# Two ways to lay 256 rows of w2 over partitions and DMA engines in a decode kernel

## The chip, the cores and the metric

The kernel runs on one core of one Trainium2 chip. The metric is the device time of one execution in microseconds (us). Before the change it is 134.84 us, the median of 6 runs between 134.77 and 134.99. The profile comes from one execution of 134.82 us; its span, from the first to the last instruction on the core, is 133.0 us. Times inside the execution are counted from the start of the span.

## What is computed

Two branches read the same layer-normalised input `xn` of shape (2, 1, 576), and their sum with the residual is the output. Branch A is attention of a single token over the last 2048 of 8192 cached positions. Branch B is a two-layer MLP with a squared ReLU.

```python
def _A_ref(x, k_cache, v_cache, wq, wo):
    W = min(4096, max(256, Sk // 4))                    # 2048
    q = (x @ wq).reshape(B, Sq, Hq, Dh) ...             # 32 heads of 128, 16 kv heads
    scores = jnp.einsum("bhqd,bhkd->bhqk", q, k) * (Dh ** -0.5)
    o = jnp.einsum("bhqk,bhkd->bhqd", _softmax(scores), v)
    return o.reshape(B, Sq, Hq * Dh) @ wo               # wo: 4096 x 576

def _B_ref(x, w1, b1, w2, b2):
    h = jnp.einsum("bsd,df->bsf", x, w1) + b1           # w1: 576 x 4608
    r = jnp.where(h > 0, h, 0)
    return jnp.einsum("bsf,fd->bsd", r * r, w2) + b2    # w2: 4608 x 576

xn = _layernorm(x)
return x + _A_ref(xn, ...) + _B_ref(xn, ...)
```

Everything is bf16. All caches and weights that are used are read once: 53.62 MB from HBM.

## The kernel before

The 2 x 16 pairs of batch and kv head are worked through in eight units `u` of four kv heads. A unit's K and its V are 2 MB each and lie in a pool of six tiles, `kvpool`, which later also holds w2. For each unit `step` (line 518) transposes K on TensorE (`transposes`, line 315, read back by ACT and DVE at lines 327 and 329), computes scores and the softmax, and does the product with V of the unit two steps earlier. After the last unit come the MLP's first layer (`mlp_h_start` to `mlp_h_end`), the last two V products, wo and w2, then the final addition (line 594) and the store (line 595).

All large loads are issued by SyncE (SP), in an order written out by hand: K of unit 0, wq, K and V of the units, then `issue_wo(0)`, w1, the last two V, `issue_wo(1)`, and w2 in six pieces (`W2P`, line 510, loaded by `issue_w2`, line 164, whose `dma_start` is line 173). An SP load is issued when its buffer is free and when an earlier DMA that used the same completion semaphore has landed; DMAs of SP and ACT take eight semaphores in turn. Each of these loads has 128 partitions, so each of the core's 16 DMA engines gets eight rows of it.

w2 has 4608 rows of 576 numbers (1152 bytes each). They are divided into four groups of `HW` = 1152 rows. In the first three groups a partition holds `FR` = 9 neighbouring rows. In the last group, 896 rows are laid over 128 partitions with `FT` = 7 rows each, and the remaining 256 rows are "extra" rows that `XS` (line 74) describes. An entry of `XS` is (rows in a partition, partitions, partitions of one DMA):

```python
    def issue_w2x():
        if x_parts:
            s, i = x_parts.pop(0)
            xr, xp, xe = XS[s]
            rows = B_w2[FX[s]:FX[s] + xr * xp, :].rearrange("(e i r) n -> i e (r n)", e=xe, r=xr)
            tc.keep_in_program_order(nc.scalar.dma_start(out=w2x_sb[s][i:xp:xp // xe, :], in_=rows[i]))
```

So an entry is loaded by xp / xe DMAs of xe partitions each, with one contiguous run of xr rows for each partition. ScalarE (ACT) issues them (line 186), one at each call of `issue_w2x`, and `load_k` and `load_v` call it from unit 3 and unit 1 on. Before the change, (3, 32, 8) makes four DMAs of 8 partitions with 3456 bytes each, and (8, 20, 5) makes four DMAs of 5 partitions with 9216 bytes each. ACT also issues the loads of x, b1 (4 partitions of 2304 bytes) and b2 (1152 bytes), and the store of the output.

The extra rows are used by `mlp_x` (line 491): two matmuls for each row index, 2 x (3 + 8) = 22 in all, which contract over 32 or 20 partitions. `mlp_h_end` (line 447) transposes the activations into the same layout, with one small transpose for each entry of `CX` (7 + 3 + 8 = 18) and one copy for each of the three layouts (line 467). The last two pieces of w2 are used by `mlp_tail` (line 479), whose result `tail_ps` goes into the final addition.

Of the kernel before, what the change touches and what calls it, by code (L numbers as in the profile page):

```python
# [16 lines left out]
def kernel(  # L17
# [53 lines left out]
    HW = F // NG4  # L71
    HB = HW // 3
    FR = HW // P
    XS = ((3, 32, 8), (8, 20, 5))
    FT = (HW - sum(r * p for r, p, _ in XS)) // P
    F3 = (NG4 - 1) * HW
    CX = [(r, FT, P) for r in range(FT)]
    FX = []
    for xr, xp, _ in XS:
        FX.append(F3 + FT * P + sum(m * n for m, n, _ in XS[:len(FX)]))  # L80
        CX += [(FX[-1] - F3 + r, xr, xp) for r in range(xr)]
    assert FX[-1] + XS[-1][0] * XS[-1][1] == F
    N3 = (NG4 - 1) * FR
# [92 lines left out]
    const.tile([P, 96], F32, name="pad_0")  # L176
    w2x_sb = [const.tile([xp, xr * D], BF16, name=f"w2x_sb_{i}") for i, (xr, xp, _) in enumerate(XS)]
    const.tile([P, 24], F32, name="pad_1")
    x_parts = [(s, i) for s, (_, xp, xe) in enumerate(XS) for i in range(xp // xe)]

# [445 lines left out]
```

## Time and profile before

| quantity | value |
|---|---|
| median of 6 runs | 134.84 us (134.77 to 134.99) |
| the profiled execution | 134.82 us, span 133.0 us |
| busy: PE / DVE / ACT / POOL | 88.7 / 58.6 / 46.9 / 5.4 us |
| bytes moved by DMA | 53.74 MB, 404 GB/s over the span |
| mean granted TensorE clock | 0.879 |
| ACT-issued DMAs for the extra rows | 4 of 45.0 KB, 4 of 27.0 KB |
| matmuls on the extra rows (`mlp_x`) | 22, from 112.0 us on, 404 to 443 ns each |
| last piece of w2: issued at, landed at | 107.59, 129.65 us |
| store of the output issued at | 130.38 us |

The busy shares of the compute engines say how much work each has, not what sets the end. For that one reads the chain of work that ended last, and then the stage in which it ends. The DMA row of the profile is a mean over 16 DMA engines that each work off their own share; the queue table names who asked for the bytes: q1 is SP's queue, q10 is ACT's, and the queues of kind "instruction" bring the engines' own program code.

### The profile page before, as it was taken

The page shows a single profiled execution, that of the slowest core. Times are in us where ns is not written, and L with a number is a line of the kernel's source. Part 1 is how long each engine was busy: PE and PEld are TensorE (multiplying, and loading weights), DVE is VectorE, ACT ScalarE, POOL GpSimd, SP SyncE. Part 2 cuts the span into 40 slices and gives each one's busy share as a digit, 9 for nine tenths or more (in the row PEclk, how much of TensorE's full clock was granted, in tenths as well). Part 3 has the DMA queues.
Part 4 walks back from the last instruction along what each step waited for, and adds up shares of the span by engine and source line. Part 5 has one row for each costly group of instructions (what it writes and reads, how often), then busy time and mean ns, then how long its engine had stood idle before and what let it go on. Part 6 is the DMA issues. An engine that isn't in the chain of part 4 may idle for free.

```text
span 133.0 us, 2082 instructions
## 1 busy us (share of the span) xinstructions
PE 88.7 (67%) x850; PEld 52.5 (39%) x850; DVE 58.6 (44%) x160; ACT 46.9 (35%) x65; POOL 5.4 (4%) x18
## 2 busy tenths in 40 slices
PE   0069546988697477678497597497815495927970
PEld 0059214465353244344253353265402153314640
DVE  6725305244584574394367584574400423062010
ACT  5717303178294256256084184463200400000010
POOL 7000000010100100100100100100100000000000
PEclk9999985569999999999999999999996865555797
DMA  4999999999999999999999999999999999999940
GB/s 124 422 417 446 424 434 433 424 429 430 419 443 412 443 428 423 434 431 426 434 424 443 424 438 424 429 438 421 432 423 433 434 432 420 433 407 436 407 184 1
DMA packets 4458, 53.74 MB, mean 404 GB/s; under 512 B 551, under 2 KB 682, under 8 KB 1230
## 3 DMA queue, kind: packets, MB, share of 16 engines
q1 hardware_dynamic: 4320, 53.32, 94.4%
q10 hardware_dynamic: 130, 0.31, 0.6%
q8 instruction: 6, 0.10, 0.3%
q14 instruction: 2, 0.02, 0.0%
HBM read 53.62 MB, written 0.00 MB: 403 GB/s over the span
## 4 chain that ended last, share of the span: by engine, by line
DMA 92%; PE 3%; DVE 1%; SPq 1%; issue 0%; DVEq 0%
DMA v<-in_A_v_cache_dram 43%; DMA k<-in_A_k_cache_dram 20%; DMA w<-in_B_w_dram 17%; DMA wq<-in_A_wq_dram 12%; PE kT_ps L110 2%; PE o_ps L107 1%; SPq L128 0%; DVE kT L329 0%; SPq L135 0%; DVE o L386 0%; DVE o L388 0%; DVE fin_sb L594 0%; PE tail_ps L107 0%; DVEq L594 0%
## 5 line engine op out<-in xcount | busy, mean ns | idle before, releaser
L110 PE MATMUL kT_ps<-ident_f,k 128*128 128x128 f32 x256 | 39.4, 298 | 12.4 <-DMA k<-in_A_k_cache_dram 9.7
L110 PEld LDWEIGHTS kT_ps<-ident_f,k 128*128 128x128 f32 x256 | 30.7, 152 | 25.8 <-issue 13.6
L327 ACT COPY kT<-kT_ps 128x1024 bf16<-128x1024 bf16 x32 | 31.7, 1013 | 19.7 <-PE kT_ps L110 18.8
L329 DVE COPY kT<-kT_ps 128x1024 bf16<-128x1024 bf16 x32 | 21.8, 682 | 16.4 <-PE kT_ps L110 16.4
L107 PE MATMUL sc_ps<-kT,qz 128*32 128x512 bf16 x128 | 10.5, 413 | 5.8 <-DVE kT L329 5.8
L359 ACT ACTIVATE p<-sc_ps,bias 128x512 bf16<-128x512 f32 x8 | 5.5, 687 | 17.9 <-DVE gown L355 14.4
L107 PE MATMUL o_ps<-v,pT 128*32 128x512 bf16 x128 | 11.2, 445 | 0.0
L588 ACT COPY part<-out_ps 17x144 f32<-17x144 f32 x2 | 0.5, 268 | 23.8 <-DVE part L588 23.8
L348 DVE TENSOR_REDUCE m<-sc_ps 128x1 f32<-128x512 f32 x8 | 5.5, 692 | 7.2 <-PE sc_ps L107 7.2
L388 DVE SCALAR_TENSOR_TENSOR o<-o_ps,in_s,o 128x128 f32<-128x128 f32 x24 | 8.3, 347 | 0.5
L362 DVE STREAM_TRANSPOSE pT<-p 128x512 bf16<-128x512 bf16 x8 | 5.7, 710 | 6.4 <-ACT p L359 6.4
L107 PEld LDWEIGHTS <-xnT 128*2 128x2 bf16 x100 | 2.6, 96 | 11.8 <-issue 10.8
L107 PE MATMUL out_ps<-wo,ws 128*17 128x288 bf16 x64 | 6.1, 365 | 1.6 <-DVE ws L421 1.6
L352 POOL PARTITION_ALL_REDUCE gmax<-m x8 | 2.9, 367 | 88.3 <-DVE m L350 88.3
L386 DVE TENSOR_SCALAR o<-o_ps,in_s 128x128 f32<-128x128 f32 x8 | 2.7, 343 | 8.6 <-PE o_ps L107 8.5
L107 PE MATMUL h_ps<-w,xnT 128*2 128x384 bf16 x48 | 3.2, 421 | 4.9 <-DMA w<-in_B_w_dram 4.9
L107 PE MATMUL op_ps<-o,of_h 128*128 128x129 f32 x16 | 4.0, 338 | 3.3 <-DVE o L388 3.2
L107 PEld LDWEIGHTS <-qz 128*32 128x32 bf16 x128 | 2.2, 98 | 10.0 <-DVE kT L329 7.4
L107 PEld LDWEIGHTS <-hT_sb 128*17 128x17 bf16 (+2 forms) x104 | 4.6, 100 | 3.7 <-issue 1.4
L453 DVE TENSOR_TENSOR hrow<-t 98x384 bf16<-98x384 f32 x3 | 1.6, 556 | 8.3 <-ACT t L452 8.2
L107 PEld LDWEIGHTS <-ws 128*17 128x17 bf16 x64 | 3.7, 112 | 3.8 <-DVE ws L421 1.9
L110 PE MATMUL pro_ps<-ident,tmp_x 2*128 2x2 bf16 x6 | 0.5, 176 | 6.6 <-DVE tmp_x L233 6.6
(79 smaller groups left out, 59.6 us busy)
## 6 DMA issues: line engine op xcount, KB each, us to landing
k<-in_A_k_cache_dram SPq DMA_DIRECT2D x8, 2048.0 KB, 23.6
v<-in_A_v_cache_dram SPq DMA_DIRECT2D x8, 2048.0 KB
wo<-in_A_wo_dram SPq DMA_DIRECT2D x2, 2304.0 KB
w<-in_B_w_dram SPq DMA_DIRECT2D x2, 2304.0 KB
wq<-in_A_wq_dram SPq DMA_DIRECT2D x2, 2048.0 KB, 16.3
w<-in_B_w_dram SPq DMA_DIRECT2D x3, 1296.0 KB
w_rem<-in_B_w_dram SPq DMA_DIRECT2D x1, 576.0 KB, 36.9
w<-in_B_w_dram SPq DMA_DIRECT2D x1, 576.0 KB
```

Source lines behind the costliest of these rows:

```text
L107: tc.keep_in_program_order(nc.tensor.matmul(*a, **k))
L110: tc.keep_in_program_order(nc.tensor.transpose(*a, **k))
L327: nc.scalar.copy(out=kT, in_=kT_ps[:])
L329: nc.vector.tensor_copy(out=kT, in_=kT_ps[:])
L348: nc.vector.tensor_reduce(out=m1[:], in_=sc_ps[:], axis=AX.X, op=ALU.max)
L352: nc.gpsimd.partition_all_reduce(gmax[:], m2[:], channels=P, reduce_op=ReduceOp.max)
L359: nc.scalar.activation(out=p_sb[:], in_=sc_ps[:], func=ACT.Exp, bias=bias[:, 0:1], scale=scale, accum_out=o1[:, Dh:Dh + 1])
L362: nc.vector.transpose(out=pT[:].rearrange("p j r -> p (j r)"), in_=p_sb[:])
L386: nc.vector.tensor_scalar(scalar1=in_s[:, 0:1], scalar2=None, op0=ALU.mult, **kw)
L388: nc.vector.scalar_tensor_tensor(scalar=in_s[:, k:k + 1], in1=o1[:, 0:Dh], op0=ALU.mult, op1=ALU.add, **kw)
L453: nc.vector.tensor_tensor(out=hrow[:, k * HB:(k + 1) * HB], in0=t1, in1=t1, op=ALU.mult)
L588: cp(out=part[32 * i:32 * i + MB, :], in_=out_ps[32 * (i // 2):32 * (i // 2) + MB, (i % 2) * OQ:(i % 2 + 1) * OQ])
```

## The change

One line is different:

```diff
-    XS = ((3, 32, 8), (8, 20, 5))
+    XS = ((10, 24, 6), (1, 16, 16))
```

The same 256 rows are now 240 rows on 24 partitions with ten rows each, and 16 rows on 16 partitions with one row each. The first entry makes four DMAs of 6 partitions with 11520 bytes each, the second a single DMA of 16 partitions with 1152 bytes each. ACT thus issues five DMAs for the extra rows instead of eight, at the first five calls of `issue_w2x`; the later calls find nothing left to load. `mlp_x` does 2 x (10 + 1) = 22 matmuls, which contract over 24 or 16 partitions. `CX` has 7 + 10 + 1 = 18 entries, and the three copies at line 467 take 7, 10 and 1 columns. In ACT's order the loads of b1 and b2 now stand behind the first four copies of K's transposes instead of ahead of them, and a few copies on DVE change places with their neighbours. SP's 30 loads stay in their order; which earlier DMA's semaphore each waits for changes, since three DMAs fewer take turns.

## The prediction

> **What bounds the kernel now.** I read the chain that ended last first, by its shares and its last links (columns: start, length, what):
>
> ```profile
> DMA 92%; PE 3%; DVE 1%; SPq 1%; issue 0%; DVEq 0%
> ...
> 107.59 22.06 DMA w<-in_B_w_dram
> ...
> 129.69 0.27 PE tail_ps L107 x4
> ...
> 130.04 0.31 DVE fin_sb L594
> ```
>
> The end is the landing of the last piece of w2 at 129.65, and 3.35 us of fixed tail behind it. That piece was issued at 107.59, so it did not lack an early issue: it stood 22 us in line. Next the queue table, and the last microseconds cut into stretches (length, then busy time and instructions of PE, PEld, DVE, ACT, POOL, the clock, the mean share of the 16 DMA engines, GB/s):
>
> ```profile
> q1 hardware_dynamic: 4320, 53.32, 94.4%
> q10 hardware_dynamic: 130, 0.31, 0.6%
> q8 instruction: 6, 0.10, 0.3%
> q14 instruction: 2, 0.02, 0.0%
> ...
> 126.00:127.00 1.00, 0.86 (x16) 0.52 (x11) 0.00 (x0) 0.00 (x0) 0.00 (x0) 1.00 0.94 377
> 127.00:128.00 1.00, 0.77 (x14) 0.65 (x15) 0.00 (x0) 0.00 (x0) 0.00 (x0) 1.00 0.68 270
> 128.00:129.00 1.00, 0.90 (x26) 0.46 (x21) 0.45 (x2) 0.00 (x0) 0.00 (x0) 1.00 0.33 120
> 129.00:130.00 1.00, 0.58 (x16) 0.24 (x11) 0.15 (x1) 0.54 (x2) 0.00 (x0) 1.00 0.03 9
> ```
>
> The DMA engines do not finish together: their share falls through 0.94, 0.68, 0.33 and 0.03. Those four stretches hold 1.98 us of work for a mean engine, so a perfect balance would end near 127.98; the last engine works on to 129.35. The time is thus set by the most loaded engine, and this change moves load between engines.
>
> **Which engine is last.** The trace records every DMA packet (start, duration, bytes, queue), without its engine. But in steady state a data packet starts 3 ns before its predecessor's recorded end, and a 16384-byte packet takes 611 ns in all places, so packets can be chained end to start. With the order of SP's loads (eight packets and a 4-byte completion each) as a check, this gives 16 chains of equal SP work (3.332 MB) and, after 6.2 us, no gap. A chain's end is its work. The packets on q10 tell the chains apart: 3456-byte ones lie on eight chains, 9216-byte ones on five of these, b1's 2304-byte ones on four of the five. I call them engines 0 to 7, 0 to 4 and 0 to 3. Where each chain ends:
>
> - engines 0 to 4 (44 extra rows each): 128.42 on engine 4; on the others 128.53, 128.65, 129.06 and 129.35. The last two also carried an 8 KB code fetch (q14, at 61.5 and 31.7).
> - engines 5 to 7 (12 extra rows each), in unknown order: 126.93; 128.20 with a 16 KB code fetch (q8) at 99.3; 128.42 with one at 116.4.
> - engines 8 to 15 (none): 126.56, 126.59, 126.60, 126.95; and 128.07, 128.24, 128.36, 128.43 with one 16 KB fetch each (49.7, 27.4, 83.5, 64.4).
>
> A code fetch is costly: its own packet, plus a delay of the packet after it. For 8 KB that was 309 and then 1144 instead of 611 ns (0.84 us in all) at 31.7, and 309 and 852 (0.55 us) at 61.5. A 16 KB one cost 1.2 to 1.4 us.
>
> The Trainium skill (Runtime: NRT & Kernel Launch, section Instruction fetch mechanics) holds such a block crossing to be mostly hidden; here the four fetched engines among 8 to 15 end 1.1 to 1.9 us behind the four others, so the trace disagrees. By that rule only the rows would count and the change would give 0.16 us whatever engine 5 carries.
>
> **The change, part by part.** Packet prices come from q10's rows: 1152 bytes took 51 ns, 2304 took 93, 3456 took 135, 9216 took 347, that is 42.3 ns for each further row. An 11520-byte packet is not in the trace; one more row than 9216 makes it 347 + 85 = 432 (two rows, 2304 bytes, more). From below, ten rows at the 16384-byte rate (607/16384 x 11520) make 427; from above, as ten single rows, 510. I take 432, by its nearest row. A data packet moves its chain on by 3 ns less than it takes, a completion by 6.
> - Engines 0 to 4: 4 x 132 + 4 x 344 + 8 x 6 = 1952 ns before; 4 x 429 + 48 + 5 x 6 = 1794 after. Saved: 0.158 us each (with 510 ns packets instead: 0.154 us worse).
> - Engine 5: 4 x 132 + 4 x 6 = 552 before, 1794 after: +1.242 us.
> - Engines 6 and 7: 552 to 54: -0.498 us. Engines 8 to 15: +0.054 us.
>
> The ends become 128.26 on engine 4, 128.37, 128.49, 128.90 and 129.19 on 0 to 3, at most 128.48 on 8 to 15, below 128 on 6 and 7. Engine 5 is the open one: 128.17, 129.44 or 129.66, for its three candidates.
>
> The fetch on the chain that ends last is not a constant either. Its program is unchanged in length but for a few instructions, so I expect both 8 KB fetches on the same engines, at a price between the two seen. At 0.84 us the last end is 129.19 (-0.16); at 0.55 us for both it is 128.90 to 128.92 (-0.45). I take -0.22, nearer to the row of that very engine, since the later of two draws counts.
>
> **What costs nothing, and under which cover.** PE: 22 matmuls before and after, 18 small transposes before and after; the recorded 2.81 us from 111.95 lie far ahead of w2's landing. If the landing moves forward, PE's cover is this wait:
>
> ```profile
> 127.23 1.27 PE L107 MATMUL out_ps<-w,hT_sb 128*17 128x288 bf16 x18 [0.37 <-DMA w<-in_B_w_dram]
> ```
>
> Up to 0.37 us PE follows; beyond that PE's own work is next, so the gain is nearly capped there. ACT: three issues fewer (631 to 752 ns each) under an engine that is 35% busy. b1 and b2 moved behind four K copies: b2 is needed after unit 1, about 40 us, b1 after 95 us. Early on, engines 0 to 5 get two packets of 429 instead of 132 ns ahead of wq, so wq and the next K land up to 0.6 us later, and the K copies, scores and buffer releases slip with them. SP is covered by the line at the DMA engines: from issue to a load's first packet it was never under 10.2 us after the first three loads, nor under 12.4 us after 45 us. SP's waits for these very loads can go too:
>
> ```profile
> SPq L128 <- DMA w2x_sb<-in_B_w_dram: 15.3, 3, 13.5
> ```
>
> but this time is waiting with a full line, worth nothing. If a wait grew by more than the 10 us, the engines would idle and every further us would cost one.
>
> The skill also advises (DMA: Bandwidth & Descriptors, Rules for kernel authors, "Use all 16 engines") against a DMA confined to c < 16 engines. An even spread of 256 rows puts 16 rows, some 0.7 us, on engines with a fetch (128.43 to 129.1) and takes 1.2 us from 0 to 3: near 129.1 as well. So the trace doesn't support that rule strongly here.
>
> **Forecast (0.62).** Engine 5 is the one without a fetch. The six 16 KB fetches went, in time, to four chains of 8 to 15, then to two of 5 to 7, to none of 0 to 4. That looks like a walk downwards; by ones it is 11, 10, 9, 8, 7, 6, and engine 5 stays free. The profiled 134.82 becomes 134.60; the median lies 0.02 above it, so 134.62, with an own range of 134.37 to 134.72.
>
> **Rival 1 (0.22): engine 5 has the last fetch.** A walk by twos (15, 13, 11, 9, 7, 5) fits as well. Then that chain goes from 128.42 to 129.66, 0.31 beyond today's 129.35: 135.15, slower. It decides as soon as engine 5 carries more than 129.35 - 128.17 = 1.18 us besides its rows. Against it stands only that a walk by ones is simpler.
>
> **Rival 2 (0.10): engine 5 has the fetch of 99.3.** 129.44, +0.09: 134.93. The two late fetches would come as 5 and one of 6 and 7, which fits no even walk.
>
> **Rival 3 (0.05): the balance moves, but code fetches move too**, as ACT's and DVE's programs are a little shorter and K copies slip. If no 8 KB fetch fell on 0 to 3, the ends would be 128.5, and PE's cover gives 0.4 to 0.8: 134.2. If both fell on one engine, it would end at 128.4 + 1.4 = 129.8: 135.2. **The split fails (0.01)**: if six partitions ran on three engines, each would carry 80 rows, 1.7 us more: 136.3. Loads of 4, 5 and 8 partitions ran on 4, 5 and 8 chains, which speaks against it.
>
> **How the numbers follow.** A change under 0.2% (0.27 us) can hardly be told from none on this kernel. The forecast is split by its fetch price: 0.22 faster, 0.40 same. Rival 1 adds 0.14 slower, 0.08 same (its 0.31 is close to the bound); rival 2 falls within, 0.08, or slower, 0.02; rival 3 adds 0.03 faster and 0.02 slower, the failed split 0.01 slower. Since the unhit case rests on an order that I only inferred, I shift some of "same" to both sides: faster 0.29, same 0.45, slower 0.26. The time is 134.62, the range 134.30 to 135.20.
>
> **What would show it.** Six chains with four 11520-byte packets each of about 432 ns; one 1152-byte packet on each of 16; the last landing 0.16 to 0.45 us earlier; the line before loads still 10 us long; three DMA issues gone from ACT. A last chain that carries 11520-byte packets, a 16 KB fetch and no b1 makes rival 1 or 2 right. Gaps in the chains after 7 us, or a longer tail than 3.35 us, would make the whole approach wrong.

## The result, and the profile after

The changed kernel takes 136.57 us, the median of 16 executions between 134.86 and 138.71; the kernel before, run beside it, takes 134.84 (134.71 to 135.13, 36 executions). The ratio is 1.0091, with a 95% interval of 1.0073 to 1.0109; it leaves out the six executions over 1.5% above the fastest, the profiled one among them, and the median does not. The change made the kernel about 1% slower, and it made its time scatter over almost 4 us where it had scattered over 0.4.

The profile after is of an execution of 137.11 us; a second one, of 137.11 us as well, is e1's below. From the page of the first: the span, the row of DMA bandwidth in 40 slices of 3.4 us, the queue table and the shares of the chain that ended last.

```profile
span 135.3 us, 2079 instructions
...
GB/s 151 393 422 441 441 415 441 431 416 434 426 431 425 443 426 426 378 363 349 395 441 426 431 431 436 417 436 436 430 423 425 441 420 441 413 420 426 409 136 1
...
q1 hardware_dynamic: 4320, 53.32, 94.1%
q10 hardware_dynamic: 106, 0.31, 0.6%
q8 instruction: 6, 0.10, 0.3%
q14 instruction: 2, 0.02, 0.0%
...
DMA 56%; PE 28%; DVE 8%; issue 2%; ACT 1%; SPq 1%; POOL 0%; ACTq 0%; DVEq 0%
```

The queues moved the same bytes as before, with 24 packets fewer on q10. The bandwidth row has what the row of before doesn't have: four slices, from the 17th on, with 378, 363, 349 and 395 GB/s between neighbours of 426 to 441. Those slices cover 54 to 68 us. The same stretch in windows of 2 us, first after, then before (length; busy time and instructions of PE, PEld, DVE, ACT and POOL; the clock; the mean busy share of the 16 DMA engines; GB/s):

```profile
52.00:54.00 2.00, 2.00 (x20) 1.18 (x19) 1.80 (x5) 1.01 (x1) 0.00 (x0) 1.00 0.99 418
...
56.00:58.00 2.00, 1.92 (x22) 1.18 (x19) 1.10 (x4) 0.00 (x0) 0.37 (x1) 1.00 0.98 352
58.00:60.00 2.00, 1.21 (x14) 0.55 (x14) 1.13 (x2) 1.95 (x4) 0.00 (x0) 1.00 0.96 344
60.00:62.00 2.00, 2.00 (x21) 1.27 (x19) 1.97 (x6) 1.67 (x2) 0.00 (x0) 1.00 1.01 360
...
66.00:68.00 2.00, 0.40 (x2) 0.43 (x3) 0.60 (x3) 0.78 (x2) 0.37 (x1) 0.81 1.00 418
```

```profile
58.00:60.00 2.00, 1.21 (x10) 0.98 (x11) 1.87 (x5) 1.25 (x2) 0.00 (x0) 1.00 1.02 435
60.00:62.00 2.00, 2.00 (x21) 1.18 (x19) 0.69 (x1) 1.08 (x2) 0.00 (x0) 1.00 0.99 421
```

The engines are as busy as ever (0.96 to 1.01), but they move less: the packets themselves are slower. From 54.7 to 65.3 us each 16384-byte packet on all 16 chains (the prediction's name for one engine's packets, one behind the other) takes about 733 ns (724 to 735) instead of 611. That is 1.20 times as long, and it costs each chain about 1.75 us. The first slow packet starts at 54.30, right behind the last of the 16 single-row packets of the new DMA, which lie at 52.9 to 54.2 us. The last slow ones are in flight when the code fetch of 8 KB starts, at 65.29. Within the stretch the 16 chains start their packets in one fixed order, with offsets that stay the same to a few ns, period after period.

The last microseconds, in the same columns as the four windows that the prediction showed:

```profile
126.00:127.00 1.00, 1.00 (x14) 0.57 (x9) 0.00 (x0) 0.00 (x0) 0.00 (x0) 0.50 1.00 420
127.00:128.00 1.00, 1.00 (x12) 0.61 (x10) 0.00 (x0) 0.00 (x0) 0.00 (x0) 0.50 0.97 396
128.00:129.00 1.00, 1.00 (x14) 0.65 (x12) 0.00 (x0) 0.00 (x0) 0.00 (x0) 0.67 0.81 324
129.00:130.00 1.00, 1.00 (x20) 0.76 (x18) 0.00 (x0) 0.00 (x0) 0.00 (x0) 1.00 0.65 252
130.00:131.00 1.00, 1.00 (x26) 0.68 (x24) 0.00 (x0) 0.00 (x0) 0.00 (x0) 1.00 0.21 78
131.00:132.00 1.00, 0.64 (x30) 0.35 (x20) 0.59 (x2) 0.19 (x1) 0.00 (x0) 1.00 0.04 15
```

The DMA share falls as it did before, about 2 us later, with a longer and thinner tail (0.65, 0.21, 0.04). PE is full too, at half the clock until 128.7. That is why the chain that ended last names PE this time, and it has to be told from a cause. The timeline of the end (start, length, what, and in brackets the idle time before it with its releaser):

```profile
127.71 3.33 PE L107 MATMUL out_ps<-w,hT_sb 128*17 128x288 bf16 x44
...
131.09 0.61 DVE L588 COPY part<-out_ps 17x144 f32<-17x144 f32 x2 [8.43 <-PE out_ps L107]
131.61 0.61 PE L107 MATMUL tail_ps<-w,hT_sb 128*17 128x144 bf16 x12 [0.29 <-DMA w<-in_B_w_dram]
131.81 0.55 ACT L588 COPY part<-out_ps 17x144 f32<-17x144 f32 x2 [24.58 <-DVE part L588]
...
132.39 0.31 DVE L594 TENSOR_TENSOR fin_sb<-tail_ps,part 113x144 bf16<-113x144 f32 x1 [0.69 <-ACT part L588]
```

The last piece of w2, issued at 109.8, landed 22.1 us later, at 131.9. Before, the addition of line 594 started 0.39 us after that landing, which would be 132.3 here; it started at 132.39. PE, which had no wait left ahead of these matmuls, thus delayed the end by about 0.1 us through ACT's copy; the other 2.25 us come from the later landing. In the second profile of this kernel (e1 below) the landing alone sets the end, at the same 137.11 us.

### The profile page after: what moved, and what is told of

Its sections match the earlier page's. It is cut to its first block, busy times and chain, and to the rows that moved or that the text cites. A ratio compares the mean times of both kernels' runs of the same rounds, so it can differ in the third digit from the quotient of the medians.

```text
span 135.3 us, 2079 instructions
## 1 busy us (share of the span) xinstructions
PE 94.0 (69%) x850; PEld 55.3 (41%) x850; DVE 58.4 (43%) x160; ACT 46.8 (35%) x65; POOL 5.4 (4%) x18
## 4 chain that ended last, share of the span: by engine, by line
DMA 56%; PE 28%; DVE 8%; issue 2%; ACT 1%; SPq 1%; POOL 0%; ACTq 0%; DVEq 0%
DMA v<-in_A_v_cache_dram 27%; DMA k<-in_A_k_cache_dram 16%; DMA wq_rem<-in_A_wq_dram 13%; PE out_ps L107 8%; PE kT_ps L110 8%; PE o_ps L107 5%; PE sc_ps L107 4%; DVE o L388 2%; DVE kT L329 1%; PE op_ps L107 1%; DVE qrow L293 1%; DVE o L386 1%; SPq L135 1%; PE qT_ps L110 1%; ACT L359 1%
## 5 line engine op out<-in xcount | busy, mean ns | idle before, releaser
L110 PE MATMUL kT_ps<-ident_f,k 128*128 128x128 f32 x256 | 43.2, 317 | 11.8 <-DMA k<-in_A_k_cache_dram 6.4
L110 PEld LDWEIGHTS kT_ps<-ident_f,k 128*128 128x128 f32 x256 | 33.3, 162 | 26.8 <-issue 10.9
L107 PE MATMUL sc_ps<-kT,qz 128*32 128x512 bf16 x128 | 11.1, 434 | 5.8 <-DVE kT L329 5.8
L107 PE MATMUL o_ps<-v,pT 128*32 128x512 bf16 x128 | 12.3, 483 | 0.2 <-DMA v<-in_A_v_cache_dram 0.2
L107 PEld LDWEIGHTS <-qz 128*32 128x32 bf16 x128 | 2.2, 99 | 10.2 <-DVE kT L329 7.6
L107 PEld LDWEIGHTS op_ps<-o,of_h 128*128 128x128 f32 x16 | 2.8, 220 | 5.0 <-DVE o L388 5.0
L107 PE MATMUL h_ps<-w,xnT 128*2 128x384 bf16 x48 | 2.3, 325 | 3.4 <-DMA w<-in_B_w_dram 3.4
```

Of the source, the lines that this page charges most:

```text
L107: tc.keep_in_program_order(nc.tensor.matmul(*a, **k))
L110: tc.keep_in_program_order(nc.tensor.transpose(*a, **k))
```

## The experiments

All ratios are against the kernel before, run beside each. Chain ends are rebuilt from the packets as the prediction describes; a chain is "fetched" when it carried a 16 KB code fetch. In the kernels with ten-row loads the packets don't tell engine 4 from engine 5, which carry the same ones; of the two chains one is fetched. Engine 4 had no 16 KB fetch in before, where the packets tell it apart, so I call the fetched one engine 5. Theories that several experiments name: M, that it matters which SBUF partitions an engine writes; R, that it matters which HBM rows are read at the same time; P16, that sixteen small packets at once are enough; T, that the place in time decides; C, that the delays which the ten-row loads give some chains are needed too.

**e1: the changed kernel again.** No edit.

> The changed kernel once more, nothing altered. In its profiled run every 16384-byte packet took 733 instead of 611 ns from 54.7 to 65.3 us, on all 16 chains at once, which cost each chain 1.75 us. Theory D (disturbance): the stretch has nothing to do with the change; then this run, beside the kernel before, is even, 134.6 to 135.2, and the trace has no such stretch. Theory P (provoked): the changed loads provoke it; then the times scatter again from 134.9 to over 137 while the kernel before stays within 134.7 to 135.1, and a stretch of 733 ns packets comes back. Theory F (fetch): the 16 KB code fetches now fall on engines 0 to 5, too (one did, at 66.4); then a chain with 11520-byte packets and a fetch ends last, some 1.4 us behind its unfetched neighbours.

136.82 us (136.41 to 137.11, 4 executions), ratio 1.0135 (1.0111 to 1.0159). Its bandwidth row:

```profile
GB/s 156 413 418 426 441 420 431 426 441 410 441 431 432 426 420 399 378 378 383 373 409 431 431 436 423 432 425 430 436 422 420 446 429 417 431 416 435 409 166 1
```

The dip is there again, with packets of 694 to 704 ns (1.15 times) from 52 to 68 us. It starts with the single-row packets at 50.3 to 51.5 and ends with the 8 KB fetch at 67.9. In both executions the last chain is one with ten-row packets, a fetch and no b1, which I call engine 5; its fetch came at 66.4 in the one and at 27.7 in the other.

**e2 and e6: the 16 rows in another shape, the ten-row loads as they are.** One line each:

```diff
-    XS = ((10, 24, 6), (1, 16, 16))
+    XS = ((10, 24, 6), (1, 16, 8))    # e2: two DMAs of 8 partitions
+    XS = ((10, 24, 6), (1, 16, 4))    # e6: four DMAs of 4 partitions
```

> As the changed kernel, but the 16 single rows are loaded by two DMAs of 8 partitions instead of one DMA of 16. If the DMA on all 16 engines, whose packets landed 1.5 us ahead of the slow stretch, provokes it (P16), this kernel is even near 134.6 to 135.3 and has no 733 ns packets. If the 11520-byte packets on six engines do (P10), it scatters to 136 and more as the changed kernel does. D and F say nothing changes against e1_repeat, within 0.1 us of load (engines 0 to 7 carry 2 rows, 8 to 15 none).

> The changed kernel, but the 16 single rows are loaded by four DMAs of 4 partitions, four apart, so that every engine writes into partitions 4e to 4e+3 only. M and P16: no slow stretch. Load: engines 0 to 3 get 4 x 429 + 4 x 48 + 8 x 6 = 1956 ns (1952 before), 4 and 5 get 1740, the others none; so 134.8 where engine 5 has no 16 KB fetch, 135.0 to 135.2 where it has one. If the stretch comes back, 136 and more, both M and P16 fall and the 11520-byte packets are left.

e2 takes 135.04 us (134.51 to 136.56, 10 executions), ratio 1.0003 (0.9991 to 1.0015); e6 takes 135.11 (134.99 to 135.30, 11), ratio 1.002 (1.0011 to 1.0029). The dip is gone, as e6's row shows:

```profile
GB/s 138 374 448 427 432 416 447 417 437 426 427 427 434 431 432 427 430 432 422 437 422 432 427 432 428 440 431 436 425 409 441 427 437 437 410 423 429 400 155 1
```

In e2 engine 5 has a fetch, at 69.6, and ends last, at 129.74; rival 1, which gave it one, had 129.66. In e6 the last chain ends at 129.73, with a fetch at 99.2. So about 1.5 us of the loss hang on the form of the one small DMA. In e6 the partitions of one DMA lie four apart, as those of the ten-row loads do; in e2 they lie two apart.

**e3 and e4: eight rows instead of ten, with and without the 16-partition DMA.**

```diff
-    XS = ((10, 24, 6), (1, 16, 16))
+    XS = ((8, 30, 5), (1, 16, 16))    # e3; e4 has (1, 16, 8)
...
-    const.tile([P, 24], F32, name="pad_1")
+    const.tile([P, 600], F32, name="pad_1")
```

> 240 rows on 30 partitions of eight rows (six DMAs on engines 0 to 4, 9216-byte packets) and the 16 rows by one DMA on all 16 engines. Engines 0 to 4 carry 49 rows instead of 44: 6 x 344 + 48 + 7 x 6 = 2154 ns against 1952 before, so +0.20 us by load alone, 135.04. P16: scatters to 136 and more, with a stretch of 733 ns packets. P10: even near 135.0. F: over 135.8 where a 16 KB fetch falls on engines 0 to 4.

> As e3, but the 16 rows by two DMAs of 8 partitions. No 16-engine DMA on ACT and no 11520-byte packet: P16 and P10 both say even near 135.1 (engines 0 to 4: 6 x 344 + 2 x 48 + 8 x 6 = 2208 ns, +0.26). A scatter here would leave neither of them. F as for e3.

137.38 us (137.18 to 137.57), ratio 1.0186 (1.017 to 1.0203), and 137.35 (137.11 to 137.76), ratio 1.0187 (1.0167 to 1.0207). Both missed, and the two don't tell the theories apart, since they changed two things that weren't meant. Partitions of one load lie six apart (30 / 5), and packets slow down while those loads run, up to 1.33 and 1.46 times (medians of 1 us). And the tiles behind them lie 64 bytes lower, after which most 16384-byte packets took 613 to 620 ns instead of 611, and most 10368-byte ones 392 to 399 instead of 389. Other partitions (e9) and a shifted address (e8 against e11) are tried singly below. In e3 the DMA of 16 partitions, at 60.5 to 61.1 us, was followed by about 1 us of packets of up to 688 ns, and by no long stretch.

**e5, e9 and e10: the kernel before, with its loads laid out differently.** e9 changes the partitions alone, e10 the rows alone, e5 both. In e9 and e10 the rows thus lie on other partitions than the matmuls take them from, which changes the result and not the sizes of the transfers.

```diff
-            rows = B_w2[...].rearrange("(e i r) n -> i e (r n)", e=xe, r=xr)
+            rows = B_w2[...].rearrange("(i e r) n -> i e (r n)", e=xe, r=xr)       # e5, e10
-            tc.keep_in_program_order(nc.scalar.dma_start(out=w2x_sb[s][i:xp:xp // xe, :], in_=rows[i]))
+            tc.keep_in_program_order(nc.scalar.dma_start(out=w2x_sb[s][i * xe:(i + 1) * xe, :], in_=rows[i]))  # e5, e9
```

> The kernel before with the same eight ACT loads (same rows, sizes, engines), but the partitions of one DMA lie side by side instead of four apart. Before, engine e always writes its extra rows into partitions 4e to 4e+3; here it writes into partition 8i+e or 5i+e of the tile. Load by chain is the same, so theory L (load and fetches alone) says 134.84, within 0.1. Theory M (map: an ACT load whose engines write other partitions than 4e to 4e+3 slows all engines, as the DMA of 16 single rows with engine e into partition e did) says 136 or more, scattered, with packets well over 611 ns after or during these loads. Theory P16 (it is the DMA on all 16 engines) says 134.84.

> Half of e5: the kernel before, the eight ACT loads read the same HBM rows in the same pattern as before, only the partitions they are written to lie side by side (the rows thus end up in other partitions than the matmuls assume). In e5 both the HBM pattern and the partitions differed. Theory M (which partitions an engine writes): 137 or more, slow packets on all 16 chains while these loads run. Theory R (which HBM rows are read together): 134.85, even, as before.

> The other half of e5: the ACT loads read neighbouring HBM rows together, as in e5, but are written four partitions apart, as before (again the rows end up in other partitions than the matmuls assume). M: 134.85, even. R: 137 or more.

e5 takes 137.52 us (ratio 1.019, 1.0173 to 1.0208), e9 137.88 (1.0223, 1.0208 to 1.0238), e10 134.83 (0.9999, 0.999 to 1.0008). The windows around two of the loads, first e9, then e10:

```profile
48.00:50.00 2.00, 1.15 (x15) 0.71 (x8) 1.60 (x5) 0.78 (x1) 0.00 (x0) 1.00 1.07 375
50.00:52.00 2.00, 2.00 (x21) 1.18 (x20) 0.99 (x2) 1.01 (x1) 0.00 (x0) 1.00 0.97 351
...
60.00:62.00 2.00, 1.69 (x13) 0.56 (x12) 0.81 (x3) 1.01 (x1) 0.00 (x0) 0.78 1.16 350
```

```profile
48.00:50.00 2.00, 1.14 (x10) 0.91 (x10) 1.87 (x5) 0.65 (x1) 0.00 (x0) 1.00 0.98 415
50.00:52.00 2.00, 2.00 (x20) 1.18 (x19) 0.73 (x2) 1.01 (x1) 0.00 (x0) 1.00 1.03 434
...
60.00:62.00 2.00, 2.00 (x20) 1.18 (x19) 0.79 (x2) 1.01 (x1) 0.00 (x0) 1.00 1.00 430
```

With the same bytes and the same engines, partitions side by side cost 3 us and neighbouring rows nothing: M holds, R falls. In e9 the packets are 1.09 to 1.48 times as long (medians of 1 us) while ACT's small loads run, on all 16 chains, also on those that carry no extra row: those without a fetch end at 128.10 to 128.32, where they ended at 126.56 to 126.96 before. A few engines that write other partitions can thus slow all the others. They need not: e2 (two apart) above and e7 and e13 (side by side) below show no slow packets. For the loads of 9216 and 3456 bytes the runs show that four apart is even, and side by side is not; six apart (e3, e4) was not either, beside shifted tiles.

The Trainium skill (DMA: Bandwidth & Descriptors, section The descriptor swizzle) states for a load of 128 partitions that engine 0 writes partitions 0 to 3 and 32 to 35, engine 1 the next four of each, and so on, one port of SBUF each. With partitions four apart, and the pieces of a load on the engines in turn, engine e's rows stay in that place; side by side they don't. This agrees with 134.83 against 137.88 us, but e7 and e13 left that place and lost at most 0.2 us; no run here shows the ports.

**e7 and e13: the kernel before with a DMA of 16 rows to 16 partitions side by side, besides its own loads,** with packets from 63.6 and from 49.7 us on. The rows are read a second time, into a tile that nothing uses:

```diff
+        if u == 4:        # e7; e13 has u == 3
+            more = const.tile([16, D], BF16, tag="row", name="more")
+            tc.keep_in_program_order(nc.scalar.dma_start(out=more[:], in_=B_w2[F - 16:F, :]))
```

> The kernel before, with one DMA more: 16 rows of w2 into 16 partitions that lie side by side, on all 16 engines, among the last loads of extra rows (their data is not used). Load: +0.054 us per engine, 134.9. M and P16: from that DMA on (some 66 to 70 us) a stretch of slow packets, 136 and more, scattered as the changed kernel. L: 134.9, even.

> e7 with the added DMA of 16 rows one unit earlier, at about 50 us, where the changed kernel has it. If its place in time decides (T): slow, 136 and more, a stretch of 700 to 733 ns packets from about 52 us. If the loads around it decide (the chains' relative delays that the ten-row loads make, C): even, 134.9 to 135.2, as e7.

135.04 us (134.86 to 135.19), ratio 1.0013 (1.0004 to 1.0022), and 135.03 (134.97 to 135.10), ratio 1.0007 (0.9998 to 1.0017). There is no dip in either, so the sixteen rows alone, in their new form and at about the time that they have in the changed kernel (from 50.3 in e1, from 52.9 in after), do not start it. T falls; C is left, with the reserve that the tile lies elsewhere in SBUF.

**e12: the changed kernel with its 16 rows spread as 144-byte pieces over all 128 partitions.** It sets the tile of the 16 rows to zero, so their product is left out. ACT also issues b1's load ahead of the ten-row loads here.

```diff
+            if s == 1:
+                more = const.tile([P, D // 8], BF16, tag="row", name="more")
+                src = B_w2[FX[s]:F, :].rearrange("a (b n) -> (a b) n", b=8)
+                tc.keep_in_program_order(nc.scalar.dma_start(out=more[:], in_=src))
+                return
```

> The changed kernel, but the DMA of 16 single rows goes as 144-byte pieces to all 128 partitions, so it still runs on all 16 engines at the same place, while each engine writes the partitions it always writes (that data is not used: the 16 rows are left out of the sum, their tile is zero). M: no slow stretch, 134.9 to 135.3, even. P16 (any DMA on all 16 engines that ACT puts between SP's): the stretch is back, 136 and more, scattered.

135.14 us (134.81 to 135.24, 10 executions), ratio 1.0013 (1.0004 to 1.0023), and no dip. Each engine gets eight small packets there instead of one, so P16 falls. Eight partitions for each engine is also how SP's loads are spread.

**e14 and e15: the 16-row DMA later, and ahead of the ten-row loads.**

```diff
-        if u >= 3:
+        if u == 3 or u == 4:              # e14, in load_k
...
-        if u >= 1:
+        if u >= 1 and u != 3:             # e14, in load_v
...
-    XS = ((10, 24, 6), (1, 16, 16))
+    XS = ((1, 16, 16), (10, 24, 6))       # e15
```

> The changed kernel with its DMA of 16 rows a unit later, at about 60 us, as in e7. T: even, near 135.1. C: a stretch of slow packets from about 62 us, up to the next code fetch (65 to 70 us), so shorter than in the changed kernel: 135.5 to 136.5, scattered.

> The changed kernel with the two entries exchanged: the DMA of 16 rows is ACT's first load of extra rows (packets at 6 us), the ten-row loads follow. If the stretch starts with that DMA and lasts until a code fetch or another ACT load moves a chain, it is short (other ACT loads follow at 9 us) or absent: 135.1, even. If any such DMA costs some 10 us of slow packets: 136 and more, stretch from 7 us on.

e14 takes 135.53 us (135.16 to 135.69, 5 executions), ratio 1.0036 (1.002 to 1.0052). The 16-row packets lie at 60.6 to 61.7, and the windows from there on are

```profile
60.00:62.00 2.00, 2.00 (x21) 1.18 (x20) 1.64 (x4) 1.01 (x1) 0.00 (x0) 1.00 1.06 443
62.00:64.00 2.00, 1.22 (x15) 0.59 (x13) 0.69 (x1) 1.01 (x1) 0.00 (x0) 1.00 1.01 377
64.00:66.00 2.00, 0.11 (x4) 0.00 (x0) 1.09 (x4) 0.03 (x1) 0.37 (x1) 0.82 0.98 397
66.00:68.00 2.00, 1.36 (x7) 1.40 (x8) 0.71 (x1) 0.94 (x3) 0.00 (x0) 0.50 1.03 442
```

The stretch moved with the DMA, with packets 1.14 to 1.15 times as long, and again ended with the 8 KB fetch, now at 64.6: 2.5 us of it instead of 11 to 16. In three profiles out of three (after, e1, e14) the stretch ends as that fetch starts. No run moves the fetch alone, so that it ends the stretch is likely and not shown.

e15 takes 135.19 us (134.68 to 136.24, 10 executions), ratio 1.0034 (1.001 to 1.0057), without a dip in its profile; the executions scatter more than e12's, so some may have had one. That the stretch wants the ten-row loads ahead of the 16-row DMA fits C.

**e8 and e11: a split made for the load of the engines.** 128 of the 256 extra rows go back to all partitions (`FT` = 8, an even share), 120 go to engines 0 to 4 with six rows in a partition, and 8 single rows go to engines 0 and 1, all four partitions apart; engine 5 gets only its even share.

```diff
-    XS = ((3, 32, 8), (8, 20, 5))
+    XS = ((6, 20, 5), (1, 8, 2))
...
-    const.tile([P, 24], F32, name="pad_1")
+    const.tile([P, 1176], F32, name="pad_1")    # e11: 1200
...
-    W2P = [(0, 0, 9), (1, 0, 9), (2, 0, 9), (3, 0, 4), (3, 4, 6), (3, 6, 7)]
+    W2P = [(0, 0, 9), (1, 0, 9), (2, 0, 9), (3, 0, 4), (3, 4, 7), (3, 7, 8)]
```

> A try at a better balance, by the prices of the chains: 128 of the extra rows become an eighth row of the 128-partition part (each engine +0.39 us), 120 go to 20 partitions of six rows (four DMAs on engines 0 to 4), 8 to 8 partitions (four DMAs of 2, engines 0 and 1), all four partitions apart. Engines 0 and 1: -0.29 us, 2 to 4: -0.50, 5 to 7: -0.16, 8 to 15: +0.39 (128.43 to 128.82 with a fetch). The last end goes from 129.35 to between 128.85 and 129.06: 134.35 to 134.55. By M it has no slow stretch; if load is not what sets the end, it stays at 134.8.

> e8 once more, with 96 bytes more of padding. In e8 (and e3, e4) a smaller activation tile had moved all large tiles down by 96 (64) bytes, and packets took 612 to 620 instead of 611 and 399 instead of 389 ns in most places, which cost some 0.8 us. With the tiles back at their old addresses the load should show: 134.35 to 134.55 (the sum written for e8). If it is 135.4 again, the address has no part in it and the balance is wrong.

e8 missed: 135.40 us (135.34 to 135.46), ratio 1.0039 (1.0025 to 1.0053). Its large tiles lie 96 bytes off their old addresses, and its packets took 611 to 620 ns instead of 611, and 398 (median) instead of 389 for 10368 bytes. e11 differs in the 24 padding numbers alone, which put the tiles back: 134.31 us (134.17 to 134.46, 5 executions), ratio 0.996 (0.9948 to 0.9973), so 0.4% below the kernel before, and below the changed one. Its last windows and the end of its chain of waits:

```profile
126.00:127.00 1.00, 0.75 (x14) 0.63 (x15) 0.00 (x0) 0.00 (x0) 0.00 (x0) 1.00 0.94 380
127.00:128.00 1.00, 0.88 (x26) 0.47 (x21) 0.43 (x2) 0.00 (x0) 0.00 (x0) 1.00 0.69 275
128.00:129.00 1.00, 0.37 (x19) 0.21 (x12) 0.17 (x1) 0.54 (x2) 0.00 (x0) 1.00 0.26 92
129.00:130.00 1.00, 0.30 (x10) 0.10 (x3) 0.31 (x1) 0.00 (x0) 0.00 (x0) 1.00 0.00 0
```

```profile
101.74 26.92 DMA w<-in_B_w_dram
128.70 0.63 PE tail_ps L107 x16
129.36 0.05 issue
129.41 0.31 DVE fin_sb L594
```

The tail of the DMA engines ends before 129: no chain goes beyond 128.72, where before it was 129.35.

## Why the prediction missed

The chains end as follows, in us. "Forecast" is from the prediction's own figures; the last column is a profile without the stretch.

```
chain                              before           forecast        after            e1               e15
engine 5 (ten rows, no b1)         128.20 / 128.42  128.17 (free)   131.59           131.64           129.71
                                                    129.66 (rival 1)
0 to 3 with an 8 KB fetch          129.06, 129.35   128.90, 129.19  130.86, 131.10   131.01, 131.31   128.81, 129.14
engine 4 (no fetch)                128.42           128.26          130.01           130.24           128.26
none of the ten rows, 16 KB fetch  128.07 - 128.43  up to 128.48    129.75 - 130.08  130.07 - 130.32  127.96 - 128.24
none of the ten rows, no fetch     126.56 - 126.96  -               128.29 - 128.66  128.37 - 128.99  126.55 - 126.90
```

- **That the most loaded engine sets the end: right.** No chain has a gap after the first loads, and in e1 the span is the last landing (131.98) and 3.3 us of tail, against 3.35 predicted. The line ahead of the engines stayed longer than 10 us after the first three loads (10.1 us at the shortest, with 10.2 before). The waits of SP behind the small loads fell, as this row of the waits of SyncE after shows (total, times, longest), from 15.3 us to 1.6 and gave nothing, as predicted:

```profile
SPq L128 <- DMA w2x_sb<-in_B_w_dram: 1.6, 1, 1.6
```

- **The packet prices: right.** 11520 bytes took 432 ns and 1152 bytes 51. (The bound from below, 427, is a slip: 611/16384 x 11520 is 430.) Engine 4, which has only these in place of the old ones, ends e15 at the forecast's 128.26.
- **That engine 5 has no code fetch: wrong.** This is the step that failed first. The prediction read the six 16 KB fetches as a walk downwards by ones, 11 to 6. After the change engines 4 and 5 carry the same packets; of these two chains one is fetched in after, e1, e2, e6, e12, e14 and e15 alike, at times between 27.3 and 99.2 us, and in before engine 4 is told apart and has none. So engine 5 has a fetch in each of these profiles, and only its turn changes. Its price, from the two chains of e15, is 1.45 us (129.71 against 128.26). Rival 1 put the time with it at 135.15 us. The kernels that keep the ten-row loads and have no dip took 135.04 (e2), 135.11 (e6), 135.14 (e12) and 135.19 (e15). A few executions of e2 and e15 took only 134.51 to 134.79; no profile shows whether engine 5 was free in them.
- **Rival 1's order: not borne out.** Its price came true, its walk downwards by twos (15, 13, 11, 9, 7, 5) didn't, in the one profile that can test it. The packets of e2 tell engines 6 and 7 apart too, and there the next fetch after engine 5's, at 83.7 us, falls on one of these two and not on a chain of 8 to 15. By e2's order engine 5 would have had the fetch of 99.3 in before, as in rival 2. The packets of before fit almost as well with that fetch on the chain that ends at 128.43 as with it on the one at 128.20, and then rival 2's sum too comes to 129.67. The order stays open.
- **That small packets cost their own duration and no more: wrong.** It was never written as a step, but the sums of all 16 chains rest on it. In its place the runs show one DMA of sixteen 1152-byte packets followed by 10.6 and 16 us in which all packets are slow. The other 1.4 us of the median, 136.57 against some 135.15, are put down to this stretch. 1.75 us off engine 5's 131.59 leaves 129.84, close to rival 1's 129.66. The range ended at 135.20 because no rival made all packets slower at once.
- **The 8 KB fetches: right.** They fell on two of engines 0 to 3 again, and in e15, without the stretch, these chains end within 0.1 us of the forecast. They would have set the end if engine 5 had been free.
- **The skill's rules.** The trace disagrees again with the rule that a block crossing is mostly hidden (Runtime: NRT & Kernel Launch, section Instruction fetch mechanics): in e1 the fetched chains without ten-row packets end at 130.07 to 130.32 and those without a fetch at 128.37 to 128.99. The rule Use all 16 engines (DMA: Bandwidth & Descriptors, section Rules for kernel authors) advises against a DMA confined to fewer engines. An even spread of all 256 rows, which the prediction put "near 129.1", was not run; with 128 rows spread evenly and the others on engines 0 to 4 (e11) the last chain ends at 128.72, earlier than in either kernel.

**What is shown of the stretch and what isn't.** Shown: it slows all 16 engines alike; it begins with the DMA of 16 partitions and moves with it (after, e1, e14); it is absent when those rows go four partitions apart (e6) or over 128 partitions (e12), and when the same form runs in the kernel before (e7, e13); and larger loads to partitions side by side slow all engines in another kernel too (e9 against e10). Argued only: that after the slow moment the chains, already spread by the ten-row loads, keep a fixed order in which they hinder each other until a fetch shifts one of them. Why such an order lasts, and why at 1.15 or 1.20 times, is open; so is why e2, two apart, had none in its profile (one of its ten executions took 136.56), and why e3's was over after 1 us. The scatter of the kernel's time, 134.86 to 138.71, fits a stretch of changing length, but only two of its executions were profiled.

## What to carry to other kernels

Where DMA engines are never idle, balance them by their chains' ends, with the code fetches in the sum, and put the extra rows on engines that have no 16 KB fetch; here 128.72 instead of 129.35 at the last chain made 0.4%. Lay small loads over partitions as the large loads lie: here that was even each time (e6, e10, e12), while one load of 18 KB laid out otherwise was followed by some 2 us lost on all engines, though not in every kernel (e7, e13). After any change of a tile's size, check whether the packets of the untouched loads still take what they took.

## What was not expected of the hardware

- One DMA of 16 packets of 1152 bytes was followed by 10.6 us (after) and 16 us (e1) in which every large packet of every engine took 1.20 and 1.15 times its usual time.
- Partitions side by side instead of four apart cost 3.05 us (e9 against e10), with the same bytes, packets and engines.
- An SBUF address 96 bytes off cost 1.09 us over 53.7 MB (e8 against e11), seen as up to 9 ns on each large packet.
- One of the ten-row chains without b1 carried a 16 KB fetch in all seven profiles of such kernels, at times from 27.3 to 99.2 us. In before and e10, where the packets tell engine 4 apart, no 16 KB fetch fell on engines 0 to 4.
